# A longer warm-up on TensorE and an earlier load of the third group's values in a kernel of linear attention and a GELU MLP

## The chip, the cores and the metric

The kernel runs on 1 core of one Trainium2 chip. The metric is the device time of one execution in microseconds (us); lower is better. All times are of single executions or medians of a few.

## What is computed

The first half is a recurrence over 768 time steps for 4 batches and 8 heads of width 48; its output, as 3072 tokens of width 384, goes through an MLP with 2048 hidden units and the exact GELU. Everything is fp32.

```python
def _attn_ref(r, k, v, w, u):
    for t in range(S):                       # S = 768, state is D x D per batch and head
        cur = einsum('bhd,bhe->bhde', u[None] * kt, vt)
        y[:, :, t] = einsum('bhd,bhde->bhe', rt, state + cur)
        state = w[None, :, :, None] * state + einsum('bhd,bhe->bhde', kt, vt)

def _moe_ref(x, w_in, w_out):                # x: 3072 x 384, hidden 2048
    h = x @ w_in
    g = 0.5 * h * (1.0 + erf(h * inv_sqrt2))
    return g @ w_out
```

## The kernel before

**Tiling.** Time is cut into 6 chunks of 128 steps, each chunk in two halves of 64, and the 8 heads into 4 pairs. A *group* is one pair in one chunk, for all 4 batches: 24 groups, `gi` from 0 to 23. The MLP is cut by chunk (512 tokens) and by 16 slices of 128 hidden units: 96 *steps*, `m` from 0 to 95. One step is `moe1` (nine matmuls of 512 columns into the bank Hp, line 649), GELU on ScalarE (line 679), a split into a high and a low part on VectorE (lines 680, 681), and `moe2` (nine matmuls into three output banks, line 692). Numbers are split into a high and a low part in the fast fp32 form (F32R), so that three products stand for one.

**The first four groups** (`first_group`, lines 577 to 590) have to be done before the first MLP step can start. For each: the r and k rows T are scaled on VectorE (line 426); `scores` and `own` (line 465) on TensorE; `select` on VectorE (line 551) copies the masked scores out of the banks A; k is scaled on GpSimd (line 433); `gains` (line 476) multiplies k and v; `state` advances the state (lines 521, 532); `old` (line 484) and `new` (line 502, after a drain on line 498) make the output in the banks Y; `keep` copies it to xx or x3 (lines 565, 566). Groups 1 to 3 begin their output with `gaps` (line 515).

**The weights** of hidden slice j are loaded to raw (`w_load`, line 365) and split by `w_split` into wh and wl: three passes on ScalarE (lines 380, 383, 386), one on VectorE (388), one on each (391, 393).

**Order.** Nothing is ordered by hand on the engines: `Plan` (lines 52 to 149) is a list scheduler that runs on the host with a modelled duration for each operation, and writes out one fixed order for each engine. `add("pe", ns, ...)` gives TensorE work with its modelled time. Where the model sees TensorE idle, it puts in matmuls on a tile of zeros: `plan.filler` of 512 columns to the bank UE, as long as 300 ns more than its 400 fit (lines 122 to 126), and later `plan.heat` of 256 columns to AE (lines 127 to 130). All of them are line 312, `heat`.

**The warm-up** (lines 314 to 320) is the first work of TensorE: HEATS = 9 matmuls of 512 columns on zeros.

**The loads** are all issued on SyncE's queue. The first 13 go in the order of the list LOADS (line 43): t*i* is T of group i, n*i* its k and v, w*j* a weight slice. `in_turn` (lines 227 to 243) makes each of the first ten wait until the load three places ahead of it has landed, and each later one until the load two places ahead has. t0 to t3 and n0 to n3 have tiles of their own. A waiting issue holds all later ones, since the queue is in order.

Of the kernel before, what the change touches and what calls it, by code (L numbers as in the profile page):

```python
# [9 lines left out]
F32 = mybir.dt.float32  # L10
# [10 lines left out]
B, H, S, D = 4, 8, 768, 48  # L21
# [17 lines left out]
LATER = 10 ** 7  # L39
FIRST, STEP, STEP_LAST = 23000, 8400, 3900  # L40
WEIGHT_AHEAD, GROUP_AHEAD, GROUP_DUE = 12500, 28000, 20000
HEATS, HEAT_NS, HEAT_ROOM = 9, 400, 300
LOADS = ("t0", "t1", "n0", "t2", "n1", "t3", "w0", "n2", "n3", "w1", "t4", "w2", "n4")
UNDERWAY, START = 2, 10
URGENT, WORTH = 1000, .5
LEEWAY, SHARE = 700, 0.9
# [5 lines left out]
class Plan:  # L52
# [9 lines left out]
    def add(self, eng, ns, at, fn, r=(), w=()):  # L62
        n = len(self.ops)
        deps = set()
        for x in r:
            deps.add(self.writer.get(x))
            self.readers.setdefault(x, []).append(n)
        for x in w:
            deps.add(self.writer.get(x))
            deps.update(self.readers.pop(x, ()))  # L70
            self.writer[x] = n
        deps -= {None, n}
        self.ops.append((eng, ns, at, fn, deps))
        self.reads.append(set(r))
# [77 lines left out]
def rwkv_gelu_mlp(tc, rkT, rkv, wuT, uN, wmlp, r, k, vT, w, u, out):  # L152
    nc = tc.nc
    with ExitStack() as ctx:
# [7 lines left out]
        def sb(shape, dt, name, pool=None):  # L162
            return (pool or wk).tile(shape, dt, name=name)
# [6 lines left out]
        AE = pso.tile([128, 2, 512], F32, name="AE")  # L170
# [34 lines left out]
        zeros = sb([128, 512], F32R, "zeros", pro)  # L205
# [4 lines left out]
        add, dma = plan.add, plan.dma  # L210
# [71 lines left out]
        for dst, src, x in ((diag2, diag, "diag"), (past2, past, "past")):  # L282
            for h in range(2):
                add("act", 280, LATER, lambda dst=dst, src=src, h=h: nc.scalar.copy(
                    out=dst[64 * h:64 * h + 64], in_=src[64 * h:64 * h + 64, 64 - 64 * h:128 - 64 * h]),
                    r=[x], w=[f"{x}2{h}"])
# [9 lines left out]
        for i in range(NP, NP + 2):  # L296
            for h in range(2):
                add("act", 520, LATER, lambda i=i, h=h: nc.scalar.copy(
                    out=flat2(T[i])[32:64, 512 * h:512 * h + 512], in_=zeros.bitcast(F32)[32:64]),
                    r=["zeros"], w=[f"T{i}"])  # L300
# [10 lines left out]
        def heat(dst, n=512):  # L311
            nc.tensor.matmul(dst, lhsT=zeros[:, 0:128], rhs=zeros[:, 0:n], start=True, stop=True)  # L312

        def warm_up():
            for n in range(HEATS):
                heat((A + [YU[:, 0], YU[:, 1]] + [AE[:, 0], AE[:, 1]])[n % 6])
            plan.filler = lambda: heat(UE[:, 1]), "O0", HEAT_NS, HEAT_ROOM
            plan.heat = lambda: heat(AE[:, 0, 0:U0], U0), 110, SHARE

        add("pe", 430 * HEATS, 10, warm_up, r=["zeros"], w=["H", "A0", "A1", "O0", "O1", "Y0", "Y1"])  # L320

# [417 lines left out]
        n1 = sb([LP, 2], F32, "n1")  # L741
        n2 = sb([1, 1], I32, "n2", cst)
# [60 lines left out]

        for n, x in enumerate(LOADS):
            at = 10 * n + 1
# [146 lines left out]
```

## Time and profile before

| | us |
|---|---|
| median of 3 runs | 491.01 (488.01 to 491.92) |
| the profiled execution, whole | 492.2 |
| its span, first to last instruction | 490.5 |
| TensorE busy in the span | 479.8 |
| VectorE busy | 265.9 |
| ScalarE busy | 174.9 |
| GpSimd busy | 64.8 |

The profiled execution lies 1.2 us over the median; 1.7 us of it lie outside the span. In the profile, PE is TensorE's matmuls and PEld its weight loads, DVE is VectorE, ACT ScalarE, POOL GpSimd and SP SyncE (SPq its queue of DMA issues). L312 is line 312 of the kernel. A busy time of PE counts matmuls that overlap once. "issue" as the cause of an idle time means that the engine waited for nothing that the profile shows.

### The profile page before, as it was taken

What the parts mean: (1) busy time and instruction counts of PE and PEld (TensorE: products, weight loads), DVE (VectorE), ACT (ScalarE), POOL (GpSimd) and SP (SyncE); (2) the same over time, 40 slices, a digit from 0 to 9 for tenths busy, and PEclk for the clock granted to TensorE, in tenths of its full rate; (3) what the DMA queues carried; (4) which work ended last, traced back from release to release, by engine and by line L of the source; (5) the groups of instructions that cost most, each with busy time, mean ns of one, the idle gap of its engine ahead of it and who ended that gap; (6) DMA issues with size and microseconds to landing.
All of it is one profiled execution on the core that took longest, in us unless ns stands there. A gap on an engine that the chain in (4) does not pass through costs nothing.

```text
span 490.5 us, 11672 instructions
## 1 busy us (share of the span) xinstructions
PE 479.8 (98%) x5094; PEld 389.8 (79%) x5094; DVE 265.9 (54%) x432; ACT 174.9 (36%) x353; POOL 64.8 (13%) x85
## 2 busy tenths in 40 slices
PE   8799999999999999999999999999999999999996
PEld 6687787878888888778878888888888887888885
DVE  7478989876636636536545645554545423322223
ACT  6288889853132232231321331331421311211111
POOL 5200000002202022112022021120120200000000
PEclk9799999999999999999999999999999999999999
DMA  8674576513312312303113403123313000100002
GB/s 221 210 234 170 176 268 198 193 37 113 91 31 62 92 34 77 131 0 94 43 49 94 143 3 94 33 60 93 103 42 94 1 11 13 66 0 0 1 0 71
DMA packets 13193, 42.25 MB, mean 86 GB/s; under 512 B 2160, under 2 KB 2544, under 8 KB 13136
## 3 DMA queue, kind: packets, MB, share of 16 engines
q1 hardware_dynamic: 13136, 41.43, 28.1%
q8 instruction: 42, 0.69, 0.6%
q14 instruction: 15, 0.12, 0.1%
HBM read 34.74 MB, written 4.72 MB: 80 GB/s over the span
## 4 chain that ended last, share of the span: by engine, by line
PE 96%; DVE 1%; issue 1%; DMA 1%; ACT 0%; SPq 0%; DVEq 0%
PE Hp L649 41%; PE O L692 40%; PE A L465 3%; PE Y L484 3%; PE Y L502 2%; PE AE L312 2%; PE Y L476 2%; PE Y L692 1%; DMA T<-in_rkT_dram 1%; DVE T L426 0%; PE Y L515 0%; PE UE L476 0%; DVE Am L551 0%; DVE wa L865 0%; PE A L312 0%
## 5 line engine op out<-in xcount | busy, mean ns | idle before, releaser
L649 PE MATMUL Hp<-xx,wh 128*128 128x512 f32 x576 | 166.6, 396 | 0.5 <-ACT gf L679 0.3
L679 ACT ACTIVATE gf<-Hp 128x512 f32<-128x512 f32 x96 | 57.4, 598 | 229.2 <-PE Hp L649 223.6
L680 DVE CAST gh<-gf 128x512 fp32r<-128x512 f32 x95 | 45.5, 479 | 168.4 <-ACT gf L679 167.6
L649 PEld LDWEIGHTS Hp<-xx,wh 128*128 128x128 f32 x576 | 106.8, 188 | 25.8 <-ACT gf L679 1.2
L649 PE MATMUL Hp<-xx,wl 128*128 128x512 f32 x288 | 83.3, 396 | 0.0
L692 PE MATMUL O<-gh,wh 128*128 128x512 f32 (+1 forms) x285 | 81.9, 394 | 0.0
L692 PE MATMUL O<-gl,wh 128*128 128x512 f32 (+1 forms) x285 | 80.7, 390 | 0.0
L692 PE MATMUL O<-gh,wl 128*128 128x512 f32 (+1 forms) x285 | 80.6, 390 | 0.0
L681 DVE TENSOR_TENSOR gl<-gf,gh 128x512 fp32r<-128x512 f32 x95 | 73.2, 771 | 9.7 <-DVE gh L680 0.5
L649 PEld LDWEIGHTS Hp<-xx,wl 128*128 128x128 f32 x288 | 54.0, 188 | 12.9
L692 PEld LDWEIGHTS O<-gh,wh 128*128 128x128 f32 x285 | 52.5, 188 | 12.6 <-issue 0.3
L692 PEld LDWEIGHTS O<-gl,wh 128*128 128x128 f32 x285 | 52.5, 188 | 11.6
L692 PEld LDWEIGHTS O<-gh,wl 128*128 128x128 f32 x285 | 52.5, 188 | 11.6
L456 ACT ACTIVATE Am<-diag,cs 128x64 f32<-128x64 f32 x120 | 31.7, 337 | 29.8 <-DVE cs L451 29.8
L430 POOL TENSOR_TENSOR Nb<-Nb 128x384 f32<-128x384 f32 x15 | 15.9, 1063 | 127.9 <-DMA Nb<-in_rkv_dram 112.7
L433 POOL TENSOR_TENSOR Nb<-Nb,WN 128x384 f32<-128x384 f32 x20 | 21.5, 1073 | 56.3 <-DMA Nb<-in_rkv_dram 32.0
L426 DVE TENSOR_TENSOR Tb<-Tb,E 112x1024 f32<-112x1024 f32 x20 | 25.2, 1258 | 3.2 <-DMA Tb<-in_rkT_dram 3.0
L521 DVE SCALAR_TENSOR_TENSOR Sb<-Sa,E,Y 48x192 f32<-48x192 f32 x40 | 16.5, 413 | 14.0 <-ACT xx L565 7.7
L493 POOL MEMSET turn<- 1x1 f32 x19 | 1.7, 89 | 129.2 <-PE Y L484 129.2
L565 ACT CAST xx<-Y 112x512 fp32r<-112x512 f32 (+1 forms) x18 | 10.6, 587 | 22.4 <-PE Y L476 16.4
L551 DVE COPY_PREDICATED Am<-past,A 128x512 f32<-128x512 uint32 x24 | 17.7, 736 | 0.4
L448 POOL TENSOR_TENSOR Nb<-Nb,u_sb 128x384 f32<-128x384 f32 x15 | 17.3, 1155 | 0.1
(109 smaller groups left out, 401.1 us busy)
## 6 DMA issues: line engine op xcount, KB each, us to landing
raw<-in_wmlp_dram SPq DMA_DIRECT2D x16, 768.0 KB, 4.3
Nb<-in_rkv_dram SPq DMA_DIRECT2D x15, 576.0 KB, 4.0
Tb<-in_rkT_dram SPq DMA_DIRECT2D x40, 192.0 KB, 3.5
out_dram<-raw SPq DMA_DIRECT2D x5, 768.0 KB, 3.8
Nb<-in_rkv_dram SPq DMA_DIRECT2D x5, 384.0 KB, 3.7
xx<-x SPq DMA_DIRECT2D x30, 64.0 KB, 2.3
N<-in_rkv_dram SPq DMA_DIRECT2D x4, 384.0 KB, 6.4
T<-in_rkT_dram SPq DMA_DIRECT2D x2, 448.0 KB, 4.8
```

The lines of the kernel that those rows point to most:

```text
L426: add("dve", sdve(1024), LATER if g.gi else -10 ** 5, lambda: nc.vector.tensor_tensor(out=flat, in0=flat, in1=E[:, 0, g.p].rearrange("l h ...
L430: add("pool", pool(DM), LATER, lambda: nc.gpsimd.tensor_tensor(out=g.n[:, 0], in0=g.n[:, 0], in1=g.n[:, 1], op=ALU.mult), r=[g.K], w=[g.R])
L433: it = nc.gpsimd.tensor_tensor(out=g.kn, in0=g.kn, in1=WN[:, g.p].rearrange("s j d -> s (j d)").unsqueeze(1).to_broadcast([C, NB, 2 * D]), ...
L448: add("pool", pool(DM), LATER, lambda: nc.gpsimd.tensor_tensor(out=g.n[:, 0], in0=g.n[:, 0], in1=u_sb[:, g.p, :].unsqueeze(1).to_broadcast ...
L456: add("act", sact(HALF) + 60, LATER, lambda x=x, b=b: nc.scalar.activation(out=g.am[:, x, b, :], in_=diag2, func=AF.Copy, scale=g.sums[:, ...
L521: return nc.vector.scalar_tensor_tensor(out=g.s[h + 1][quarter(1 - x)], in0=g.s[h][l], scalar=E[l, 1, g.p, h, MID:MID + 1], in1=gained(g, ...
L551: add("dve", 722, LATER, lambda: nc.vector.copy_predicated(out=g.am, mask=mask.bitcast(U32).unsqueeze(1).unsqueeze(1).to_broadcast([C, 2, ...
L649: nc.tensor.matmul(O[3], lhsT=wt[j][:, 0, k_ * 128:(k_ + 1) * 128], rhs=x[:, a, k_, :], start=start and k_ == ks[0], stop=stop and k_ == k ...
L679: add("act", 600, LATER, lambda: nc.scalar.activation(out=gf, in_=O[3], func=AF.Gelu), r=["H"], w=["gf"])
L680: add("dve", sdve2(512), LATER, lambda: nc.vector.tensor_copy(out=high, in_=gf), r=["gf"], w=[GH])
L681: add("dve", sdve(512), LATER, lambda: nc.vector.tensor_tensor(out=low, in0=gf, in1=high.bitcast(F32), op=ALU.subtract), r=["gf", GH], w=[GL])
L692: nc.tensor.matmul(bank(dst)[:, a:b], lhsT=wt[j][:, 1, d * 128:(d + 1) * 128], rhs=gt[:, a:b], start=(j == 0 and n == 0), stop=(j == NJ - ...
```

## The change

The warm-up has seven matmuls of 512 columns in place of nine, and after them 26 small matmuls of zeros: 64 rows by 64 weight columns by 16 columns, in true fp32, which take turns over the four 64 by 64 quarters of the array and write to the bank AE. The scheduler's modelled time of the warm-up goes from 430 x 9 = 3870 ns to 430 x 7 + 40 x 26 = 4050 ns. In LOADS, n2 and w0 change places.

```diff
-HEATS, HEAT_NS, HEAT_ROOM = 9, 400, 300
-LOADS = ("t0", "t1", "n0", "t2", "n1", "t3", "w0", "n2", "n3", "w1", "t4", "w2", "n4")
+HEATS, SMALL, HEAT_NS, HEAT_ROOM = 7, 26, 400, 300
+LOADS = ("t0", "t1", "n0", "t2", "n1", "t3", "n2", "w0", "n3", "w1", "t4", "w2", "n4")
...
         def warm_up():
             for n in range(HEATS):
                 heat((A + [YU[:, 0], YU[:, 1]] + [AE[:, 0], AE[:, 1]])[n % 6])
+            z = zeros.bitcast(F32)
+            for n in range(SMALL):
+                i, j = (slice(64 * (n // k % 2), 64 * (n // k % 2) + 64) for k in (1, 2))
+                nc.tensor.matmul(AE[j, n % 2, 0:16], lhsT=z[i, 0:64], rhs=z[i, 0:16], start=True, stop=True)
...
-        add("pe", 430 * HEATS, 10, warm_up, r=["zeros"], w=["H", "A0", "A1", "O0", "O1", "Y0", "Y1"])
+        add("pe", 430 * HEATS + 40 * SMALL, 10, warm_up, r=["zeros"], w=["H", "A0", "A1", "O0", "O1", "Y0", "Y1"])
```

## Rows read from the trace of the kernel before

**Rows 1.** The page: busy times and instruction counts; queue of instructions (packets, MB, share).
```profile
PE 479.8 (98%) x5094; PEld 389.8 (79%) x5094; DVE 265.9 (54%) x432; ACT 174.9 (36%) x353; POOL 64.8 (13%) x85
...
q8 instruction: 42, 0.69, 0.6%
```

**Rows 2.** Windows: us, PE, PEld, DVE, ACT, POOL busy (count), clock, DMA share, GB/s.
```profile
0.00:10.16 10.16, 8.45 (x93) 6.20 (x97) 7.12 (x20) 6.87 (x15) 5.10 (x13) 1.00 0.78 213
0.00:13.34 13.34, 11.07 (x221) 8.41 (x221) 10.13 (x24) 8.41 (x19) 7.09 (x14) 1.00 0.83 230
16.38:23.20 6.82, 6.40 (x117) 5.70 (x117) 1.92 (x3) 1.39 (x3) 1.97 (x2) 0.50 0.59 181
35.20:490.50 455.30, 450.76 (x4443) 365.57 (x4443) 243.73 (x390) 155.63 (x316) 54.77 (x68) 1.00 0.25 75
```

**Rows 3.** Timeline of PE to the first step: start, length, what, [idle before].
```profile
1.57 1.22 PE L312 MATMUL A<-zeros 128*128 128x512 f32 x2 [1.57 <-DVE E L331]
...
5.58 1.36 PE L312 MATMUL UE<-zeros 128*128 128x512 f32 x4
6.86 0.69 PE L465 MATMUL A<-T 48*64 48x64 f32 x32
...
11.60 0.65 PE L465 MATMUL A<-T,KB 48*64 48x64 f32 x32
12.07 0.61 PE L484 MATMUL Y<-T,Sb 48*48 48x64 f32 x16
12.78 0.55 PE L502 MATMUL Y<-Am,N 64*48 64x64 f32 x24
16.80 0.46 PE L502 MATMUL Y<-Am,N 64*48 64x64 f32 x8 [3.46 <-issue]
17.19 2.07 PE L312 MATMUL AE<-zeros 128*128 128x256 f32 x8
19.19 1.13 PE L465 MATMUL A<-T 48*64 48x64 f32 x32
20.10 1.08 PE L465 MATMUL A<-T,KB 48*64 48x64 f32 x32
21.11 1.43 PE L312 MATMUL AE<-zeros 128*128 128x256 f32 x5
22.47 0.88 PE L476 MATMUL UE<-N 64*48 64x48 f32 x32
23.28 1.22 PE L312 MATMUL AE<-zeros 128*128 128x256 f32 x8
24.43 0.69 PE L465 MATMUL A<-T 48*64 48x64 f32 x32
...
30.96 0.54 PE L476 MATMUL UE<-N 64*48 64x48 f32 x32
31.44 1.46 PE L312 MATMUL AE<-zeros 128*128 128x256 f32 x10
...
35.17 0.47 PE L649 MATMUL Hp<-xx,wh 128*128 128x512 f32 x1
```

**Rows 4.** DMA view, 14.5 to 15.6: the instruction queue's first packet.
```profile
q8 instruction: 1, 0.02, 5.6%
```

**Rows 5.** Timeline of SP's DMA issues: w0, then n2 and n3, then w1.
```profile
9.91 0.35 SPq L365 DMA_DIRECT2D raw<-in_wmlp_dram  x1
10.95 2.48 SPq L261 DMA_DIRECT2D N<-in_rkv_dram  x2
18.10 0.33 SPq L365 DMA_DIRECT2D raw<-in_wmlp_dram  x1
```

**Rows 6.** Timelines of POOL, DVE and ACT: who takes the loads up.
```profile
19.13 1.97 POOL L433 TENSOR_TENSOR N<-N,WN 128x384 f32<-128x384 f32 x2 [6.14 <-DMA N<-in_rkv_dram]
...
10.93 1.21 DVE L426 TENSOR_TENSOR T<-T,E 112x1024 f32<-112x1024 f32 x1
...
24.09 0.91 ACT L383 ACTIVATE wb<-raw 128x768 uint32<-128x768 uint32 x1
```

## The prediction, written before the changed kernel was seen

> **What bounds the kernel now.** I read the page first: PE is busy 479.8 of 490.5 us [rows 1]. Then the busy times by stretch: from 35.2 us to the end PE is busy 450.76 of 455.30 us [rows 2], so that nothing which the change could touch there is worth a microsecond, and whatever the first 35 us lose or win arrives at the end whole. Then the timeline of PE in these 35 us. It has one hole: 24 of the 32 matmuls of `new` of group 0 run from 12.78 on, and the other eight come at 16.80, after 3.46 us idle that the profile puts to "issue" [rows 3]. They are one burst of one function with the same inputs; no data can be missing between the 24th and the 25th. What can be missing is the instruction itself. The instruction queue moved 42 packets with 0.69 MB, 16.4 KB each [rows 1], and its first packet lies between 14.5 and 15.6 us, inside the hole [rows 4]. Up to the hole PE has issued 221 matmuls and 221 weight loads [rows 2], 442 in all; the remaining 2 x 5,094 - 442 = 9,746 over 42 packets are 232 for each, somewhat more with the semaphores and drains that these counts leave out: I take 250. So PE seems to start with nearly two blocks in hand, and to run dry at the end of the second.
>
> The hole has a second price. The granted clock is 1.00 up to it and 0.50 (1.2 in place of 2.4 GHz) from 16.38 to 23.20 [rows 2]. In 17.19 to 24.43 PE works without a gap [rows 3], so this stretch is paid in full. At the full clock, with prices from the same rows: eight fillers 1.15 (23.28 to 24.43, 0.144 each), `scores` and `own` 0.47 each (11.60 to 12.07), five fillers 0.72, `gains` 0.48 (30.96 to 31.44), eight fillers 1.15: 4.44 against 7.24, **2.8 us**. Hole and half clock together are 3.46 + 2.8 = 6.3 us.
>
> **The warm-up.** Out: two matmuls of 512 columns. Nine took 5.58 - 1.57 = 4.01 us [rows 3], 0.446 each, so 0.9 us; that spacing is about 512 columns at 1.2 GHz, the half clock, though the clock column shows 1.00 there. In: 26 matmuls in true fp32. `scores` has 16 matmul calls in the code and shows 32 matmuls [rows 3], and as many weight loads, so one call is four instructions: 26 x 4 = 104, less 2 x 2, **100 more**. Their price is shown by no row; the nearest are the bursts on quarters of the array at the half clock, 32 matmuls in 0.91 (19.19 to 20.10) and in 0.81 (22.47 to 23.28) [rows 3], 25 to 28 ns each. 52 of them are 1.4 us. Lower end, the full clock's 0.48 for 32: 0.8. Upper end, no overlap, twice the row: 2.9. I take 1.4, since shape and quarters are those of the rows. The warm-up then ends at 1.57 + 7 x 0.446 + 1.4 = 6.1 in place of 5.6; the four fillers behind it at the 0.23 that a matmul of 512 columns takes at full clock (0.9 us; the model, with 180 ns more, may drop one) end at 7.0, and `scores` of group 0 starts there in place of 6.86. Alone that is a loss of 0.15 us, or of 1.6 at the upper end.
>
> **What the 100 do to the fetch.** If the third block is asked for when PE enters the second, about 190 instructions in, that moment was 10.16 (93 + 97 issued, [rows 2]), and PE went on 16.80 - 10.16 = 6.6 us later. Now 14 + 104 + 8 + 64 = 190 are reached at the end of group 0's `scores`, near 7.5. The same 6.6 us bring the block at 14.1. PE runs dry at the 442nd instruction, which is the one that was 342nd: about half-way through `own` of group 1, near 11.85. The hole is then 14.1 - 11.85 = 2.3 us, lies a little earlier, and `new` of group 0 ends at 14.1 + 0.2 (rest of `own`) + 1.3 (12.07 to 13.34) + 0.15 (the last eight) = 15.75 in place of 17.19: 1.4 us won. The loss of 0.15 is in that. If the shorter hole, followed at once by work, leaves the clock at 1.00, the 2.8 come on top: **4.2 us**. Both ends: the hole is as long as before (nothing won) or gone (6.3).
>
> A rule speaks against this. The Trainium skill, page "Runtime: NRT & Kernel Launch", section on instruction fetch mechanics, says that blocks are 256 instructions and that crossing one is mostly hidden, and it gives TensorE room for 2048. The block agrees with the 250 above; the room does not, since the hole stands at 442. By that rule the hole would be no matter of fetching, and 100 instructions would bring nothing: 492.2.
>
> **Is the rest ready by then?** `scores` of group 2 needs T2, scaled by DVE at 10.93 to 12.14 [rows 6], and A free from group 1's `select`, two passes on DVE behind `own` of group 1; both have until 15.75 + 1.15 = 16.9. The weights' first pass on ACT starts at 24.09 because ACT's fixed order has it behind group 1's state; moved up by 4.2 it starts at 19.9, and w0 landed at 18.1 (w1's issue waits for it, [rows 5]). From 24.43 to 35.17 the order stays, so the first step moves up as a whole. That stretch has a few microseconds of waiting fillers, and the model may place these and some bursts otherwise; I cost that at nothing with 1 us either way (seven fillers).
>
> **The loads.** n2 now goes at 9.91 and w0 at 10.95, w1 waits for n2 in place of w0, and n3 stays third. What it wins: k of group 2 is scaled at 19.13 after 6.14 us of waiting [rows 6]; its `gains` run after 24.43, five microseconds later, so this was covered, and with everything moved up by 4 to 6 it is just about covered still. What it costs: w0 (768 KB, 8.2 us from issue to landing) lands some 1 to 1.5 us later, 19.1 to 19.6, still ahead of 19.9. On POOL the scaling of group 2 moves ahead into an idle time of 6 us. I take nothing for this edit, but it leaves w0 with under a microsecond of cover.
>
> **Sum.** 492.2 (490.5 and 1.7 outside) - 4.2 = 488.0 against the profiled execution. That one is 1.2 above the median, and the half-clock stretch is the likeliest thing to differ from execution to execution; half of the 1.2 taken off gives **487.4**.
>
> **The rivals.**
> *The fetch comes in time.* The 6.6 us hold 4.4 us before the packet moves, with the DMA engines full (share 0.78 to 10.16, 0.83 to 13.34, [rows 2]). If that wait was bad luck of the moment, no hole is left: 492.2 - 6.3 + 0.15 = 486.05, or 485.4 against the median. For it: no other burst in the trace waits so for the 41 other packets. Against: the DMA engines are as full at 7.5.
> *The hole keeps its length.* The fetch is sent only when PE has run dry (the packet lies 1.2 us after the hole's start), or the hole has another cause. Then it moves 100 instructions ahead with 3.46 us and the half clock behind it: 491 to 492. For it: the second block was entered at 10.16 and nothing moved before 14.5.
> *w0 comes too late (slower).* The load behind the fetch's engine was held: w0 landed 8.2 us after its issue. With the fetch asked for 2.7 us earlier, T2, k of group 1 and T3 stand where w0 stood; each late landing holds the issue of the load three places on. If T2 lands 3.4 us later, n2 goes at 13.3, w0 at 14.3 and lands at 14.3 + 8.2 = 22.5: the weights' first pass then starts at 22.5, not 19.9, and the gain is 1.6 us. It turns into a loss where w0 lands after 24.09; with k of group 2 and the fetch ahead of it by another 3.4 it would be 25.9, and 494.0.
>
> **Chances.** My forecast (486 to 489.5, the upper end by 1.6 more in the warm-up) 0.42; in time (485 to 486) 0.24; same length (490 to 492) 0.22; w0 late 0.12, of which half slower than 492. A tail of the planner's order lies in each. Range 484.9 to 491.7. About 1% (4.9 us) is what a measurement of this kernel can tell from no change: faster means under 486.1, which takes most of the second case and a little of the first, 0.29; slower means over 495.9, the worst of the last, 0.05; within 0.66.
>
> **What would show it.** Right: in PE's timeline the hole stands in `own` of group 1 (line 465), near 11.9, and is shorter than 3.46; the instruction queue's first packet lies near 12; the clock column shows 1.00 from 16 to 23 us; the first matmul of line 649 stands near 31, and 35.2 us to the end keeps its 455 us. The small matmuls take 1.4 us and `scores` of group 0 starts near 7.0. Wrong: a hole of 3.4 us at the new place (fetch sent when dry), or in `new` of group 0 as before (no fetch); a clock of 0.50 behind a shorter hole; ACT waiting on raw ahead of line 383; or a longer stretch after 35 us, which would be a fetch at another place, since all 41 later block ends move by 100 instructions as well.

## The result: 0.75% slower

| | median us | runs |
|---|---|---|
| before | 489.50 | 12, from 487.38 to 491.92 |
| changed | 493.71 | 12, from 491.20 to 496.50 |

The ratio is 1.0075, 95% interval 1.0051 to 1.0100: by it the change costs 3.7 us (the two medians lie 4.2 us apart). I had forecast 487.4 and a range up to 491.7. The profiled execution of the changed kernel has a span of 492.0 us and took 493.68, close to its median. That of the kernel before took 492.2, which is more than any of these 12 runs (in later series the same kernel took up to 493.9), so the two profiles differ by 1.5 us only, and the pages by themselves understate the loss.

The timeline of PE in the changed kernel, up to its first MLP step (start, length, what, idle before; what was line 465 is now 469, 476 is 480, 502 is 506, 649 is 653 and 692 is 696):

```profile
4.86 1.68 PE L320 MATMUL AE<-zeros 64*64 64x16 f32 x52
6.47 2.07 PE L312 MATMUL UE<-zeros 128*128 128x512 f32 x4
8.47 1.13 PE L469 MATMUL A<-T 48*64 48x64 f32 x32
...
14.32 1.10 PE L469 MATMUL A<-T 48*64 48x64 f32 x32
15.20 1.08 PE L469 MATMUL A<-T,KB 48*64 48x64 f32 x32
...
16.99 0.66 PE L506 MATMUL Y<-Am,N 64*48 64x64 f32 x32
...
18.73 0.69 PE L469 MATMUL A<-T 48*64 48x64 f32 x32
19.25 0.63 PE L469 MATMUL A<-T,KB 48*64 48x64 f32 x29
20.72 0.33 PE L469 MATMUL A<-T,KB 48*64 48x64 f32 x3 [0.84 <-issue]
...
34.50 0.47 PE L653 MATMUL Hp<-xx,wh 128*128 128x512 f32 x1
```

The hole in `new` of group 0 [rows 3] is gone: its 32 matmuls run in one piece at 16.99. A smaller hole of 0.84 us has come up in `own` of group 2. The four fillers behind the small matmuls take 2.00 us, 0.50 each, which is the half clock, where they took 1.28 before. PE stays at the half clock to about 16 us: the 32 matmuls of `scores` of group 1 take 0.88 us (14.32 to 15.20), against 0.91 at half clock in [rows 3], and those of group 2 take 0.52 (18.73 to 19.25); the clock column shows 1.00 for this stretch, as it does for the warm-up of the kernel before. The first step starts at 34.50 in place of 35.17, 0.67 us earlier. So far this is a small gain. It is lost further on:

```profile
48.72 0.63 PE L506 MATMUL Y<-Am,Nb 64*48 64x64 f32 x32
49.17 0.34 PE L480 MATMUL Y<-Nb 64*48 64x48 f32 x12
51.48 0.47 PE L480 MATMUL Y<-Nb 64*48 64x48 f32 x20 [1.97 <-issue]
```

This is the same kind of hole, 1.97 us in the middle of 32 like matmuls, in the *burst* of small matmuls of a later group (`old`, `scores`, `own`, `new`, `gains` in one piece, 320 instructions in 2.4 us). The kernel before has no such hole there (49.83, 32 matmuls in one piece):

```profile
49.83 0.54 PE L476 MATMUL Y<-Nb 64*48 64x48 f32 x32
```

The windows of the changed kernel show what it means for the second part, and what the DMA engines do ahead of the hole (columns as in [rows 2]):

```profile
34.50:492.00 457.50, 451.03 (x4443) 365.50 (x4443) 242.37 (x390) 155.99 (x316) 55.01 (x68) 1.00 0.25 75
...
46.50:49.25 2.75, 2.75 (x140) 2.32 (x140) 2.68 (x5) 1.71 (x3) 0.09 (x1) 1.00 0.96 317
```

From the first step to the end 457.5 us pass, where 455.3 passed before, with the same 4443 matmuls and 451.0 against 450.8 us of busy PE. The difference is idle time. And in the 2.75 us up to the hole the DMA engines are 96% busy: SP had just issued a weight slice.

```profile
45.68 2.05 SPq L369 DMA_DIRECT2D raw<-in_wmlp_dram  x2
49.79 0.59 SPq L848 DMA_DIRECT2D u_sb<-in_uN_dram  x1
```

The first of these two is the seventh slice, w6, 768 KB. Its packets fill the engines from 46.5 to 49.2. The instruction packet that ends the hole starts at 49.29 (DMA view, 49.25 to 49.6):

```profile
q8 instruction: 1, 0.02, 16.5%
```

### The profile page after: what moved, and what is told of

It reads as the page before. It is cut to its first block, busy times and chain, and to the rows that moved or that the text cites. A ratio compares the mean times of both kernels' runs of the same rounds, so it can differ in the third digit from the quotient of the medians.

```text
span 492.0 us, 11773 instructions
## 1 busy us (share of the span) xinstructions
PE 482.6 (98%) x5145; PEld 391.4 (80%) x5145; DVE 264.6 (54%) x432; ACT 175.1 (36%) x353; POOL 64.1 (13%) x85
## 4 chain that ended last, share of the span: by engine, by line
PE 98%; issue 1%; DVE 0%; ACT 0%
PE Hp L653 41%; PE O L696 40%; PE A L469 4%; PE Y L488 3%; PE Y L506 2%; PE Y L480 2%; PE AE L312 1%; PE Y L696 1%; PE UE L312 1%; PE A L312 1%; PE UE L480 0%; PE Y L519 0%; PE AE L320 0%; DVE wa L869 0%; PE Y L312 0%
```

## The experiments

**How to count.** In the trace of the kernel before, PE runs dry in the start after 449 matmuls, weight loads, semaphores and drains, and I put the block ends 256 apart: at 449 - 256 = 193, 449, 705 and so on. The traces bear that out: all 39 holes of PE that the 14 profiles put to "issue" begin exactly at such a count. A long burst has 320 instructions (groups 5 to 8, near 48, 66, 85 and 104 us). Where a block end lies less than 64 instructions into it, the next one lies in the same burst, and a whole block is used up in 2 us. In the kernel before that is so in one of the four (37 in, at 103.7 us), and the hole there is 0.39 us. In the changed kernel it is so in the burst at 47.3 (23 in).

The theory of the *block ends* says that the loss is this hole, and that its place follows from the number of instructions ahead. Its rivals: the *cold start* (the small matmuls leave the clock at half) and the *loads* (w0 behind n2).

**The loads alone.**
```diff
-LOADS = (... "t3", "w0", "n2", "n3", ...)
+LOADS = (... "t3", "n2", "w0", "n3", ...)
```


> The kernel before with n2 and w0 changed over in LOADS, nothing else (the scheduler then puts in one filler more, two instructions). Theory of the block ends: the change loses because 100 instructions in front move every later block end of TensorE's code, one of them into a burst; this kernel is then as fast as before, 489.5 within 1. Theory of the cold start: the small matmuls leave the clock at half to 16 us; here also no change. Theory of the loads: w0 behind n2 costs; here 493 to 494.

Measured 489.46 against 490.28 for the kernel before, ratio 0.9991 (0.9964 to 1.0017). The loads are out. The profile was worth more than the time: PE's order is that of the kernel before up to one filler, and still the start is not the one that I had argued from. Waits of PE (engine, line, for what: total, times, longest):

```profile
PE Y L502 <- issue: 1.3, 1, 1.3
...
PE UE L476 <- issue: 0.4, 1, 0.4
```

The hole in `new` of group 0 is 1.31 us, not 3.46, the clock stays at 1.00, and the first step starts at 31.81 us, not 35.17.

**The warm-up alone.** The changed kernel with the old order of LOADS; so are all further ones whose warm-up is changed, but for the two that say "the changed kernel".


> The changed kernel with the old LOADS: the new warm-up alone. Theory of the block ends and theory of the cold start: all of the loss stays, 493.5 within 1, with a hole of about 2 us in line 480 near 49 us, or the half clock up to some 16 us, or both. Theory of the loads: 489.5.

494.69, ratio 1.0089 (1.0062 to 1.0117): all of the loss is in the warm-up. The hole of 2.23 us stands in line 480, at 46 us.

**100 instructions that are not in the start.**
```diff
 for k_ in range(3):   # the first step, line 649
     ... product1(x, j, n, (k_,), ...) for n in range(3)]
+    + [k_ < 2 or late_small()]   # 26 small matmuls on zeros; the fillers behind are left out
```


> The kernel before with its old warm-up and loads; the 26 small matmuls stand behind the first step's line 649 instead, where three fillers of 512 columns are left out for them: 98 instructions more from 37 us on, none ahead of that. Block ends: a hole of about 2 us in the burst near 48 to 50 us, and 491.5 in place of 489.5. Cold start: as before, 489.5, no hole.

493.59, ratio 1.0076 (1.0046 to 1.0106). The old warm-up, the old loads, and the loss of the change all the same. The timeline of PE, and a window (columns as in [rows 2]):

```profile
46.46 0.36 PE L476 MATMUL Y<-Nb 64*48 64x48 f32 x14
48.91 0.69 PE L476 MATMUL Y<-Nb 64*48 64x48 f32 x18 [2.09 <-issue]
49.53 1.65 PE L700 MATMUL O<-gl,wh 128*128 128x512 f32 x3
50.98 1.48 PE L649 MATMUL Hp<-xx,wh 128*128 128x512 f32 x3
```

```profile
48.97:52.38 3.41, 3.41 (x25) 2.62 (x26) 2.09 (x4) 2.74 (x5) 0.00 (x0) 0.50 0.13 45
```

The hole is there, 2.09 us, and here it has a tail: behind it the granted clock is 0.50 for 3.41 us, and three matmuls of 512 columns take 1.45 us (49.53 to 50.98) where they take 0.7 at full clock. In this profile the tail and the added work cost some 0.7 us besides the hole (454.0 against 451.2 in the table below). By the ratio the run lost 3.7 us, more than the 2 that I expected; where the rest of that lies is not shown.

**The count put back.** The changed kernel with 39 small matmuls more at the same place in the first step, so that 252 instructions are added in all and the later block ends stand nearly where they were.


> The changed kernel with 39 small matmuls more behind the first step's line 649, in place of three fillers: 150 instructions more, so that with the 102 of the change all later block ends stand again within a few instructions of where the kernel before has them. Block ends: the hole near 49 us is gone and the time falls by 1.5 to 2 us, to 492. Cold start: stays at 493.7 or a little above for the added work (1 us).

491.56, ratio 1.0028 (1.0004 to 1.0053): 2.3 us of the changed kernel's loss are gone, by added work (the two intervals just touch). No hole in the burst, and the second part is back at 455.5 us (timeline of PE, then the window from the first step to the end):

```profile
13.39 0.39 PE L469 MATMUL A<-T,KB 48*64 48x64 f32 x10 [0.86 <-issue]
...
18.91 0.33 PE L469 MATMUL A<-T,KB 48*64 48x64 f32 x3 [1.74 <-issue]
...
21.25 1.86 PE L312 MATMUL AE<-zeros 128*128 128x256 f32 x8
23.05 0.69 PE L469 MATMUL A<-T 48*64 48x64 f32 x32
...
49.08 0.54 PE L480 MATMUL Y<-Nb 64*48 64x48 f32 x32
```

```profile
33.90:489.40 455.50, 451.35 (x4518) 366.25 (x4518) 243.16 (x390) 155.56 (x316) 54.64 (x68) 1.00 0.26 75
```

Its start has the code of the changed kernel, but in this profile PE is at full clock when group 0 begins (four fillers in 1.14 us, 6.12 to 7.26). It shows one way in which the start gained nothing: `own` of group 1 has a hole of 0.86 us, at the place that I forecast, and `own` of group 2 has another of 1.74, at the next block end. Together 2.6 us. Behind the second the clock is at half again: eight fillers take 1.80 us (21.25 to 23.05) where [rows 3] have 1.15 at full clock.

**Nine matmuls and 25 small ones.**
```diff
-HEATS, SMALL, ... = 7, 26, ...
+HEATS, SMALL, ... = 9, 25, ...
```


> Nine warm-up matmuls of 512 columns as in the kernel before and 25 small ones behind them (100 instructions more in front), old LOADS. Cold start: with the nine back, the granted clock is 1.00 from some 6 us on as in the kernel before, and the first step (line 653) starts 1 to 2 us ahead of that of the changed kernel in runs that are alike. Block ends: the hole of 2 us in line 480 behind 45 us stays whatever the warm-up is, and the time is 493 to 494.

493.35, ratio 1.0052 (1.0023 to 1.0082). The hole (2.2 us in line 480, with the half clock for 3.4 us behind it) does not care about the warm-up, as expected. But the start does not gain by it either: the full clock is there by 7.3 us, as expected, and still there are holes of 0.30 and 2.01 us and the first step is at 33.79, not 1 to 2 us ahead.

**Seven matmuls and no small ones.**
```diff
-HEATS, SMALL, ... = 7, 26, ...
+HEATS, SMALL, ... = 7, 0, ...
```


> Seven warm-up matmuls and no small ones, old LOADS: four instructions fewer than the kernel before. Block ends: block ends stand where the kernel before has them, no hole near 46 to 50 us, 489.5 to 490.5. Cold start: the half clock lasts as long as in the changed kernel and the time is 491 or more.

489.90, ratio 0.9999 (0.9977 to 1.0021). No hole near 46 to 50 us, no loss. By itself that says little on the cold start, since in this profile the full clock is there before 7 us. What speaks against it as the cause of the loss is the run with 98 instructions, which loses as much with the old warm-up, and the run without w6 below, which keeps the new warm-up and shows no loss.

**48 instructions.** Nine matmuls and 12 small ones.
```diff
-HEATS, SMALL, ... = 7, 26, ...
+HEATS, SMALL, ... = 9, 12, ...
```


> Nine warm-up matmuls and 12 small ones, 48 instructions more in front, old LOADS. Block ends: by the count of instructions none of the four long bursts between 40 and 105 us then has two block ends in it; no hole behind 38 us, not the 0.46 us one of the kernel before at 105.8 either, and the hole of the start comes 48 instructions earlier and is shorter: 488 to 489.5. If only the number added mattered, half of the loss: 491.5.

488.96 against 490.60, ratio 0.9982 (0.9962 to 1.0002). The block ends lie 79, 145, 193 and 247 in, none under 64. Its timeline of PE, then the window from the first step to the end:

```profile
14.26 0.66 PE L506 MATMUL Y<-Am,N 64*48 64x64 f32 x31 [0.78 <-issue]
...
30.66 0.47 PE L653 MATMUL Hp<-xx,wh 128*128 128x512 f32 x1
...
45.32 0.54 PE L480 MATMUL Y<-Nb 64*48 64x48 f32 x32
```

```profile
30.66:486.10 455.44, 450.82 (x4443) 365.33 (x4443) 244.44 (x390) 155.85 (x316) 55.08 (x69) 1.00 0.26 77
```

No hole in a burst, one of 0.78 us in the start, and one of 0.43 us among the large matmuls of a step (line 653, 48.92 us), at a block end too. Half of the instructions do not cost half of the loss; they cost nothing. The interval just reaches 1, so that this is the best of the versions tried, but no proven gain over the kernel before.

**198 instructions behind the start.** As with 98, but `late_small` makes 51.


> The kernel before with 51 small matmuls behind the first step's line 649 in place of three fillers: 198 instructions more from 35 us on. Block ends: by the count, the burst near 45 us has its block end 183 instructions in and no second one, so its hole is gone; the burst near 82 us (85.1 in the kernel before, where the block ended 239 instructions in) has one 41 in and the next 297 in, so a hole stands in line 476 near 84 us. 490.5 to 492.5. If the added work itself or its place was the loss in the run with 98: a hole near 46 us again or a loss twice as large, 496.

490.98, ratio 1.0012 (0.9985 to 1.0040). The hole near 46 us is gone and the time is that of the kernel before, though twice the work was added: neither the work nor its place was the loss. But the hole that I expected in the fourth part of the burst near 85 us (block ends 41 and 297 in) is under 0.2 us; the 32 matmuls there are spread over 0.84 us (87.58 to 88.42) in place of 0.47. A block within a burst is not enough for 2 us.

**The same burst without the load.** In the changed kernel, w6 cut to 16 columns.
```diff
-nc.sync.dma_start(raw[j % 3].rearrange("p h n t -> p (h n t)"), wbits[:, j])
+n = 16 if j == 6 else 4 * DM
+nc.sync.dma_start(raw[j % 3].rearrange("p h n t -> p (h n t)")[:, 0:n], wbits[:, j, 0:n])
```


> The changed kernel, but of the seventh weight slice (w6) only the first 16 of 1536 columns are loaded, 8 KB in place of 768, so the output is that of a stale slice; order and waits stay. Late fetch by a full queue: the 2 us hole in line 480 near 49 us is there because the block's fetch waits behind w6 on the DMA engines; without that load it shrinks to under 0.6 us, as in the bursts near 104 us where no load is on the way, and the time falls to 491.5 to 492.5. If a block that lies whole in a burst is enough for the hole: it stays at 2 us, 493.5.

490.59, ratio 1.0013 (0.9990 to 1.0037). PE's timeline at the same place:

```profile
47.56 0.34 PE L481 MATMUL Y<-Nb 64*48 64x48 f32 x12
48.49 0.47 PE L481 MATMUL Y<-Nb 64*48 64x48 f32 x20 [0.58 <-issue]
```

The same break, after the same twelve matmuls, is 0.58 us long. The instruction packet starts 0.44 us after the burst's begin (45.70 to 46.14) and not 1.99 (47.30 to 49.29): the other 1.4 us were the fetch's wait behind w6. By the two ratios the time fell by 3.0 us, more than the 1.2 to 2.2 that I expected: the hole's 1.4, and perhaps the half clock behind it in some executions, which is not shown here.

**Fewer loads under way.** As with 48 instructions, but on the chip each early load waits for the one two places ahead; the scheduler's order is unchanged.
```diff
+    near = landing[-2] if behind else None
...
-    after(x, behind[1])
+    after(x, near[1])
```


> Nine warm-up matmuls and 12 small ones (old LOADS) as in the run with 48 instructions, and each of the first ten loads waits on the chip for the load two places ahead, not three; the scheduler's order is left as it was. Late fetch by a full queue: the first hole, 0.78 us in the run with 48, goes under 0.5 us, and with fewer loads queued the first step starts as early (30.7 us) or earlier: 488 to 489. If the loads are what the start waits for: ACT, DVE or POOL waits for DMA grow by 0.5 to 1 us each and the time is 489.5 to 490.5.

491.75, ratio 1.0015 (0.9989 to 1.0041), slower than I expected on either theory. The holes in the start shrink to 0.29 us, as expected of a fetch that waits in a shorter queue; the price is that the loads come later. Waits of all engines in its first 34 us, then the same row of the run with 48 instructions:

```profile
POOL N L438 <- DMA N<-in_rkv_dram: 9.8, 3, 5.4
...
ACT wb L388 <- DMA raw<-in_wmlp_dram: 4.2, 2, 3.8
DVE xx L571 <- ACT xx L570: 3.6, 1, 3.6
...
PE Y L520 <- DVE xx L571: 2.3, 1, 2.3
```

```profile
POOL N L437 <- DMA N<-in_rkv_dram: 5.6, 3, 4.2
```

ACT waits 3.8 us for the second weight slice, ACT's part of `keep` comes behind it, VectorE's part waits 3.6 us for that, and PE 2.3 us for VectorE. Behind PE's wait its clock is at half (the four matmuls of `gaps` take 1.00 us, 30.19 to 31.19, in place of 0.57). The rival held in kind and cost more than I gave it.

**Is it the seven?** Two counterparts: nine and 25 in front with the 39 behind, and seven and 13 in front.


> Nine warm-up matmuls and 25 small ones in front (old LOADS), and 39 small ones more behind the first step in place of three fillers: the counterpart, with a full warm-up, of the changed kernel with 150 instructions more. No hole behind 38 us in either. If the weak warm-up costs in the start (half clock to 10 us and more in some executions): 490 to 490.5, over 1 us under the 491.6 of the counterpart. If the start is the same with both: 491 to 492.

> Seven warm-up matmuls and 13 small ones in front (old LOADS), 48 instructions more: the counterpart, with the weak warm-up, of the kernel with nine and 12 (489.0). No hole behind 38 us but the short one. If the weak warm-up costs in the start: 490 to 491. If not: 488.5 to 489.5.

The first: 493.00, ratio 1.0063 (1.0044 to 1.0083), which I had not expected on either theory. Its timeline says why:

```profile
105.86 0.45 PE L480 MATMUL Y<-Nb 64*48 64x48 f32 x23
107.64 0.31 PE L480 MATMUL Y<-Nb 64*48 64x48 f32 x9 [1.33 <-issue]
```

My 150 did not put the count back well enough: in the burst at 104 us the block ends lie 47 and 303 in, and a hole of 1.33 us stands there with hardly a load under way. The 37, 41 and 35 of the kernel before, of the one with 150 and of the one with seven left 0.39, some 0.2 and under 0.2 us at the same burst. So the start is not separated by this pair, and the hole fits the count. The second: 490.11, ratio 1.0000 (0.9977 to 1.0023), 1.1 us over its counterpart and in the range that I gave for a cost of the weak warm-up, but with intervals that overlap. Its start has four holes, 3.8 us in all, at full clock. Whether the warm-up costs something in the start stays open.

**All profiles in one table.** Us. The last matmul is the last of five at the very end (line 863 or its like); both times are of starts. Holes under 0.15 us are not counted.

| kernel | holes of "issue" ahead of the first step | first step | from it to the last matmul | hole in a burst behind |
|---|---|---|---|---|
| before | 3.46 | 35.17 | 451.2 | 0.39 |
| loads alone | 1.31, 0.44, 0.19 | 31.81 | 450.7 | none |
| 98 behind the start | 1.56, 0.53 | 31.64 | 454.0 | 2.09 |
| 198 behind the start | 3.61, 0.44 | 34.91 | 451.8 | under 0.2 |
| changed | 0.84 | 34.50 | 453.3 | 1.97 |
| warm-up alone | none | 31.29 | 453.3 | 2.23 |
| changed and 150 | 0.86, 1.74 | 33.90 | 451.6 | 0.2 |
| w6 cut | 0.56, 1.20, 0.84 | 32.90 | 452.0 | 0.58 |
| nine and 25 | 0.30, 2.01 | 33.79 | 454.6 | 2.2 |
| seven | 1.29 | 33.19 | 450.9 | under 0.2 |
| nine and 12 | 0.78 | 30.66 | 451.3 | none |
| fewer loads under way | 0.29 | 34.13 | 453.4 | 0.35 |
| nine and 25, 39 behind | 0.67, 2.01, 0.72 | 34.93 | 452.6 | 1.33 |
| seven and 13 | 0.25, 1.30, 1.11, 1.10 | 33.66 | 450.7 | none |

## Why the prediction was wrong

**That the hole is a late fetch, asked for before PE runs dry: right.** With 100 instructions in front the first packet starts at 10.4 to 11.0 us in six profiles (14.58 before, [rows 4], and 12.3 to 14.5 in the three others with the old warm-up), and where there is a hole in `own` of group 1 it starts 1.7 us or more after the packet. The hole is 0.30 to 0.86 us where it is there at all; I had forecast 2.3. That the fetch is asked for just when PE enters the second block is not shown. My 250 instructions per packet were near the 256 that the holes give, but not by my working: the 44 semaphores, drains and the like that I had left out add about one to the 232. I had weighed a rule against this. The Trainium skill, page "Runtime: NRT & Kernel Launch", section on instruction fetch mechanics, gives TensorE room for 2048 instructions, blocks of 256, and crossings that are mostly hidden. Against the room, PE ran dry after 449; the blocks fit all the holes; and the kernel before shows a hole at two of some 40 crossings. Those that are not hidden are worth up to 3.6 us each.

**The size of what there was to win: wrong.** I took hole and half clock from one execution, 3.46 + 2.8 = 6.3 us. That execution was slower than all 12 that were timed beside the changed kernel. Four profiles with the old warm-up start the first step at 35.17, 31.81, 31.64 and 34.91, with first holes of 3.46, 1.31, 1.56 and 3.61 us. I noted that the profile lay 1.2 us over the median and took off half of that; the place where it was slow was the very place that I priced.

**"Is the rest ready by then?": the step that failed in the start.** I asked after T2, A and w0, and not after the next block, the fourth. Its fetch went out 2.4 us and more after the first hole's end, and its first instruction too comes 100 instructions earlier. In four of the six profiles with 100 or 102 instructions in front (changed and 150, w6 cut, nine and 25 with and without the 39) it is late in `own` of group 2 by 1.20 to 2.01 us, and the holes of the start sum to 2.3 to 3.4, about the old one. I had also counted on a full clock behind the shorter holes. In the other two the holes are small (0.84 and none), but there PE is at half clock to about 16 us (changed) and 10 us (warm-up alone: `scores` of group 0 in 1.06 us, `own` in 0.62), comes to the block ends later, and pays for the warm-up directly: in the changed kernel `new` of group 0 ends at 17.58, where I had 15.75. Of the six, only the warm-up alone starts the first step where I forecast it, near 31 (31.29). The six start it at 33.6 on average, the four with the old warm-up at 33.4. The spread within each set, over 3.5 us, is far larger than that.

**"35.2 us to the end keeps its 455 us": wrong, and with it the sign.** I took it that nothing behind the start could change by a microsecond; I wrote that all 41 later block ends move and put no price on it. The price was in the trace: a burst of 320 instructions in 2.4 us (from 47.96 on), against 250 per packet, with a weight slice issued 1.6 us ahead of it (SP's issues, kernel before):

```profile
46.34 2.05 SPq L365 DMA_DIRECT2D raw<-in_wmlp_dram  x2
```

The 100 moved a block end from 125 instructions in to 23 in, and the next one into the same burst. Measured 2.0 to 2.2 us where the forecast had nothing, and some 0.7 and 1.2 more in the two profiles (98 behind the start, nine and 25) where the clock fell behind it.

**The warm-up's own cost.** 52 matmuls in 1.61 us (4.86 to 6.47), 31 ns each, where I took 1.4 us. `scores` of group 0 starts at 8.47, not 7.0, because the fillers ahead of it still ran at half clock, and I had priced them at the full one. The 1.6 us by which it comes late against the kernel before are the upper end that I gave, but by luck: that end stood for dearer small matmuls, and I had no price for a clock that stays down. It does not always: in two other profiles of the same warm-up (changed and 150, w6 cut) the four fillers take some 1.2 us.

**The loads: right.** Nothing.

What stays open: of the 3.7 us, the hole and its tail are 2.0 to 3.5 by the profiles (w6 cut: 3.0 of time). Whether the rest is lost in the start can't be told from profiles that scatter by 3.5 us there.

## What to carry to other kernels

A burst that uses a whole block of instructions in less time than a fetch takes is a place where adding or taking away instructions *anywhere ahead* can cost microseconds. Count the instructions to each burst before such an edit, and look at what the DMA engines carry just then. And before a stall of one profile is priced, see whether the stall is as long in a second execution.

## What the runs showed of the hardware

- A fetch of instructions (16.4 KB) waited behind a load that was already under way: with w6 under way the packet started 2.0 us after the burst's begin (47.30 to 49.29; 2.0 to 2.1 in the three other profiles with the long hole), at the end of a stretch in which the load kept the DMA engines 96% busy; with w6 cut it started 0.44 us after it. From the packet's start to PE's next matmul it was 2.2 to 2.5 us in all five.
- The sequencer seems to run some 40 instructions ahead of PE at the bursts: block ends 35 to 41 in gave holes of 0.4 us and less at idle DMA engines, one 47 in gave 1.33. In the kernel before and in the one with 150 more (37 and 41 in) the packet had started 0.17 and 0.28 us ahead of the burst, in that with 47 in 1.27 us after its begin. That is read from five profiles, not tested by itself, and the run with w6 cut does not fit it: 23 in, nearly idle engines, and a hole of 0.58.
- A hole of 2.1 and one of 2.2 us in a stretch of dense matmuls were followed by a granted clock of 0.50 for 3.41 us in two profiles, and holes of 1.97 and 2.23 us by no drop in two others.
